# Moving the scores of one chunk between two FFN units, and spreading block loads over the first tile

## The chip, the cores and the metric

The kernel runs on one core of one Trainium2 chip. The metric is the device time of one execution in microseconds (us). Every run also has its span (first to last instruction of the core, about 1.7 us less than the time) and its mean granted TensorE clock, 1.000 being full speed. The views name the engines thus: PE is TensorE's matrix multiplication and PEld its weight load, DVE is VectorE, ACT ScalarE, POOL GpSimd, and SPq the queue of SyncE from which the transfers (DMA) are issued. PSUM is the memory in which the kernel places PE's products; a bank is here one buffer of its PSUM pools (the pool of scores and states has four).

## The reference

Retention attention over 8 batches, 8 heads, 576 positions and 64 columns, whose output becomes a 4608 x 512 matrix, followed by a maxout feed-forward network (FFN) with three weight matrices of 512 x 768 and one of 768 x 512. The FFN weights are float64.

```python
ret = scores * Dmat[None]                 # scores = q k^T / 8, Dmat: gamma_h ** (i - j), causal
x = (ret @ v).transpose(0, 2, 1, 3).reshape(4608, 512)
h = np.maximum(np.maximum(x @ w1, x @ w2), x @ w3)
return (h @ w_out).astype(np.float32)
```

## The kernel before

The tokens are cut into 36 chunks of 128 positions and into tiles of four chunks. While the FFN of tile t runs, the attention of tile t+1 is woven into it, at twelve numbered places: at each place some attention steps are emitted, then one FFN unit (a third of the products for a pair of feature blocks).

Tile 0 is special. Its units use plain products ("up"), and beside them the float64 weights are turned into float32: DVE and ScalarE take the bit patterns apart, GpSimd (POOL) makes the last product. A piece is one block of 128 x 512 weights. Conversion runs about one unit ahead of PE, and weight bits are fetched six pieces ahead. Each POOL product is followed by the load of a later piece:

```python
w_sb[piece] = ...
nc.gpsimd.tensor_tensor(w, mant[:], expo[:].bitcast(FP32), op=ALU.mult)
load_weights(1)                     # into the same queue as everything else
```

From chunk 7 on, q and k come in as blocks of 32 x 32, which DVE transposes (for chunk 7 in 0.70 and 0.66 us). That takes 32 small loads of 16 KB for each chunk, all emitted in `load(g)`:

```python
for n, src in () if g < BY_PE else (("q", q), ("kx", k)):
    t = raws[n, g] = raw.tile([P, NP, C // 32, 32], FP32, ...)
    for blk in range(C // 32):
        for a in range(4):
            nc.sync.dma_start(t[32 * a:32 * a + 32, :, blk, :], src[...])
```

The places in tile 0, for chunks 4 and 5 (`a`, `b`), and the rule for 6 and 7 that follows at places 6 to 11:

```python
if a == CPT:
    at(0, (load, b))
    at(1, (load, a + 2))
    at(2, (transposes, b), (decay_values, b))
    at(3, (scores, a), (scores, b), (load, b + 2))
    at(4, (state, a))
    at(5, (state, b))
    at(6, (values, a, b))
    continue
at(m, (transposes, a), (decay_values, a), (load, a + 2))
at(m + 1, (transposes, b), (decay_values, b))
at(m + 2, (scores, a), (scores, b), (load, b + 2))
# state a, state b, values a, b at m + 3, m + 4, m + 5
```

`scores` takes two of the four PSUM banks of one pool and two mask copies on DVE; `state` takes one bank of the same pool. After the ninth unit come four "down" products of six blocks each with w_out, then tile 1, whose units use fewer products and prepared sums.

Of the kernel before, what the change touches and what calls it, by code (L numbers as in the profile page):

```python
# [34 lines left out]
FP32 = mybir.dt.float32  # L35
# [7 lines left out]
C = 128  # L43
NT = 4 * C
NH = NT // 2
BY_PE = 7
# [5 lines left out]
def kernel(  # L52
# [15 lines left out]
    P = 128  # L68
# [3 lines left out]
    NP = H // 2  # L72
    NG = B * S // C
    NDC = DM // P
    NF = DF // P
    CPT = NT // C
# [3 lines left out]
    raw = ctx.enter_context(tc.tile_pool(name="raw", bufs=AHEAD + 1))  # L80
# [46 lines left out]
    raws, vds, qks, sts, states = {}, {}, {}, {}, {}  # L127

    def spans(g):

        row = 0
        while row < C:
            b, pos = divmod(g * C + row, S)
            n = min(C - row, S - pos)
            yield row, b, pos, n
            row += n

    def load(g, *between):
        rows = (("k", k), ("q", q), ("v", v)) if g < BY_PE else (("k", k), ("v", v))
        for n, src in () if g < BY_PE else (("q", q), ("kx", k)):  # L140

            t = raws[n, g] = raw.tile([P, NP, C // 32, 32], FP32, tag=n, name=n + "raw", bufs=3 if n == "q" else 2)
            for blk in range(C // 32):
                b, pos = divmod(g * C + 32 * blk, S)
                for a in range(4):
                    nc.sync.dma_start(
                        t[32 * a:32 * a + 32, :, blk, :],
                        src[b, a // 2::2, pos:pos + 32, 32 * (a % 2):32 * (a % 2) + 32].rearrange("p j i -> j p i"))
        for n, src in rows:
            if n == "v":  # L150
                for t, what in between:
                    nc.sync.dma_start(t[:], what)
            t = raws[n, g] = raw.tile([C, H, D], FP32, tag=n, name=n + "raw", bufs=4 if n == "k" else 3)
            for row, b, pos, m in spans(g):
                nc.sync.dma_start(t[row:row + m], src[b, :, pos:pos + m, :].rearrange("h p d -> p h d"))
# [398 lines left out]

    warm(6)
    load(0)
    load(1, (gs, state_decay), (gq, out_decay))
    load(2)
    load(3)
    load_weights(2)  # L560
# [30 lines left out]
    def steps(t):  # L591


        todo = [[] for _ in range(3 * CPT)]

        def at(n, *what):
            todo[n].extend(partial(step, *chunks) for step, *chunks in what if max(chunks) < NG)

        for n in range(0, CPT, 2):
            a, b, m = CPT * t + n, CPT * t + n + 1, 6 * (n // 2)  # L600
            if a == CPT:
                at(0, (load, b))
                at(1, (load, a + 2))
                at(2, (transposes, b), (decay_values, b))
                at(3, (scores, a), (scores, b), (load, b + 2))
                at(4, (state, a))
                at(5, (state, b))
                at(6, (values, a, b))
                continue
            at(m, (transposes, a), (decay_values, a), (load, a + 2))  # L610
            at(m + 1, (transposes, b), (decay_values, b))
            at(m + 2, (scores, a), (scores, b), (load, b + 2))
            at(m + 3, (state, a))
            at(m + 4, (state, b))
            at(m + 5, (values, a, b))
        return todo

    for t in range(N // NT):
        work = ffn(t)
        for todo in steps(t + 1):  # L620
            for step in todo:
                step()
            next(work, None)
# [51 lines left out]
```

## Time and profile before

| | before |
|---|---|
| median of the first three runs | 823.48 us |
| those three runs | 821.67, 823.48, 825.85 |
| time of the profiled execution | 826.78 us |
| its span, mean clock | 825.1 us, 0.996 |
| PE busy | 816.1 us (99%) |

A busy share of 99% does not say that PE runs at its pace: a matmul at half clock is also busy (from 38.25 to 41.66 us of this profile PE is busy for 3.41 of 3.41 us, at clock 0.50). What matters is where PE is idle, which clock it has afterwards, and which wait ends the idle time.

### The profile page before, as it was taken

Reading aid. Unit: us, or ns where it says so; the run is one execution under the profiler, and the core shown is the slowest. Engines: PE = TensorE matmul, PEld = TensorE weight load, DVE = VectorE, ACT = ScalarE, POOL = GpSimd, SP = SyncE. Lnnn points to the kernel's source line nnn. Section 1 sums busy time; section 2 is a strip of 40 time slices with the busy share of each in tenths; the row PEclk is TensorE's granted clock in tenths of the full one; section 3 lists DMA queues with packets and bytes.
Section 4 is the critical chain, followed back from the end, with each engine's and each line's share of the span. In section 5 each row is a group of like instructions: output and inputs, shape, how many; then the busy total and the mean of one; then the engine's idle time right before and its main releaser. Section 6 shows DMA issues by size and latency. Waiting matters only on the chain.

```text
span 825.1 us, 12666 instructions
## 1 busy us (share of the span) xinstructions
PE 816.1 (99%) x4616; PEld 672.7 (82%) x4616; DVE 433.2 (52%) x805; ACT 173.7 (21%) x401; POOL 191.3 (23%) x182
## 2 busy tenths in 40 slices
PE   9899999999999999999999999999999999999998
PEld 8455546888888888888888888888888888888887
DVE  4999977555353544453544445453545344533342
ACT  2766521111111102111111111111111021111211
POOL 3645468211310130111221121202111302111000
PEclk9999999999999999999999999999999999999999
DMA  9965441333233222432233413333323223001001
GB/s 244 289 176 166 101 98 48 57 56 57 83 57 56 54 63 52 80 55 59 58 55 55 86 52 57 55 56 85 58 54 56 63 52 77 1 14 39 1 1 51
DMA packets 236094, 59.33 MB, mean 72 GB/s; under 512 B 217088, under 2 KB 234496, under 8 KB 236032
## 3 DMA queue, kind: packets, MB, share of 16 engines
q1 hardware_dynamic: 235888, 58.53, 31.4%
q8 instruction: 36, 0.59, 0.3%
q14 instruction: 26, 0.21, 0.1%
q10 hardware_dynamic: 144, 0.00, 0.0%
HBM read 49.03 MB, written 9.44 MB: 71 GB/s over the span
## 4 chain that ended last, share of the span: by engine, by line
PE 88%; DVE 6%; DMA 2%; issue 2%; ACT 1%; SPq 0%; POOL 0%; DVEq 0%; POOLq 0%; ACTq 0%
PE x L456 31%; PE z L456 15%; PE dx L329 10%; PE y L456 8%; PE dz L329 5%; PE s L186 4%; PE o L221 4%; PE o L229 3%; PE kv L200 3%; PE dy L329 3%; PE down L505 2%; DVE expo L408 2%; DMA bits<-in_moe_w_out_dram 2%; DVE frac L397 1%; DVE mant L403 1%
## 5 line engine op out<-in xcount | busy, mean ns | idle before, releaser
L456 PE MATMUL x<-S,T 128*128 128x256 f32 x576 | 147.9, 379 | 0.0
L456 PEld LDWEIGHTS x<-S,T 128*128 128x128 f32 x576 | 109.1, 190 | 15.4 <-ACT u L461 0.3
L206 POOL TENSOR_TENSOR state<-state,gs 128x512 f32<-128x512 f32 x24 | 32.3, 1345 | 242.9 <-DVE state L205 239.0
L456 PE MATMUL x<-xT,w 128*128 128x256 f32 x288 | 75.6, 385 | 0.0
L486 DVE TENSOR_TENSOR tmp<-x,p 128x256 f32<-128x256 f32 x48 | 20.4, 424 | 103.5 <-PE x L456 103.5
L456 PE MATMUL x<-S,w 128*128 128x256 f32 x288 | 74.3, 380 | 0.0
L456 PE MATMUL z<-S,w 128*128 128x256 f32 x288 | 73.9, 379 | 0.0
L456 PE MATMUL z<-xT,T 128*128 128x256 f32 x288 | 73.9, 379 | 0.0
L456 PE MATMUL y<-xT,w 128*128 128x256 f32 x288 | 73.9, 379 | 0.0
L307 POOL TENSOR_TENSOR H<-h 128x256 f32<-128x256 f32 x24 | 20.6, 858 | 226.5 <-DVE h L499 226.5
L461 ACT COPY p<-x 128x256 f32<-128x256 f32 x72 | 26.8, 373 | 202.3 <-PE x L456 202.3
L514 PE MATMUL up<-xT,w 128*128 128x512 f32 x144 | 65.3, 609 | 2.2 <-POOL w L414 2.2
L233 DVE TENSOR_TENSOR xT<-o,gq 128x512 f32<-128x512 f32 x36 | 24.7, 691 | 71.8 <-PE o L229 64.9
L456 PEld LDWEIGHTS z<-S,w 128*128 128x128 f32 x288 | 54.7, 190 | 7.4
L456 PEld LDWEIGHTS y<-xT,w 128*128 128x128 f32 x288 | 54.7, 190 | 7.4
L456 PEld LDWEIGHTS z<-xT,T 128*128 128x128 f32 x288 | 54.5, 189 | 7.7
L456 PEld LDWEIGHTS x<-S,w 128*128 128x128 f32 x288 | 49.4, 189 | 13.2 <-issue 1.5
L456 PEld LDWEIGHTS x<-xT,w 128*128 128x128 f32 x288 | 52.1, 190 | 8.0 <-issue 0.5
L514 PEld LDWEIGHTS up<-xT,w 128*128 128x128 f32 x144 | 27.3, 194 | 35.3 <-issue 31.7
L189 DVE TENSOR_TENSOR st<-s,causal 128x512 f32<-128x512 f32 x72 | 44.8, 682 | 9.1 <-PE s L186 8.2
L461 ACT COPY u<-x 128x256 f32<-128x256 f32 x72 | 26.8, 372 | 100.2 <-PE x L456 95.7
L329 PE MATMUL dx<-To,H 128*128 128x256 f32 x192 | 44.2, 380 | 0.0
(92 smaller groups left out, 1200.6 us busy)
## 6 DMA issues: line engine op xcount, KB each, us to landing
bits<-in_moe_w_dram SPq DMA_DIRECT2D x18, 512.0 KB, 5.2
out_dram<-osb SPq DMA_DIRECT2D x35, 256.0 KB, 2.1
kraw<-in_k_dram SPq DMA_DIRECT2D x32, 256.0 KB, 3.0
vraw<-in_v_dram SPq DMA_DIRECT2D x32, 256.0 KB, 3.5
qraw<-in_q_dram SPq DMA_DIRECT2D x464, 16.0 KB, 1.8
kxraw<-in_k_dram SPq DMA_DIRECT2D x464, 16.0 KB, 1.8
bits<-in_moe_w_out_dram SPq DMA_DIRECT2D x6, 512.0 KB, 6.9
qraw<-in_q_dram SPq DMA_DIRECT2D x6, 256.0 KB, 4.9
```

The costliest lines, as they stand in the source:

```text
L186: nc.tensor.matmul(s[j][:, p, :], lhsT=kT[r, p, :], rhs=qT[r, p, :], start=True, stop=True)
L189: nc.vector.tensor_tensor(st[:, j], s[j][:], masks[start_of(g)][:].unsqueeze(1).to_broadcast([C, NP, C]), op=ALU.mult)
L200: nc.tensor.matmul(kv[:, p, :], lhsT=pair(kr, p)[r:], rhs=pair(vds[g], p)[r:], start=True, stop=True)
L206: nc.gpsimd.tensor_tensor(t[:], t[:], gs[:], op=ALU.mult)
L221: nc.tensor.matmul(o[g][D * j:D * (j + 1), p, :], lhsT=vr[:, 2 * p + j, :], rhs=st[:, j, p, :], start=(p == 0), stop=(before(g) == 0 and p ...
L229: nc.tensor.matmul(o[g][:, p, :old], lhsT=sd[:, p, :], rhs=qT[:, p, :old], start=False, stop=(p == NP - 1), skip_group_check=True)
L233: nc.vector.tensor_tensor(xT[t][:, :, i * C:(i + 1) * C], o[g][:], gq[:], op=ALU.mult)
L307: chores.append(lambda: (pool(s3, a11, a21, op=ALU.subtract), pool(s4, a12, s2, op=ALU.subtract)))
L329: nc.tensor.matmul(out[m], lhsT=hS[n](fp)[:, m * P:(m + 1) * P], rhs=late["T"][n][:, fp, :], start=first and fp == 0 and (m == 0 or last a ...
L456: nc.tensor.matmul(out[:], lhsT=w[:, d * P:(d + 1) * P], rhs=xS[t][n][:, d, :], start=first and d == 0, stop=d == 1, skip_group_check=True)
L461: nc.scalar.copy(c[:], src[:])
L514: nc.tensor.matmul(ps[:], lhsT=w_sb[i, fb][:, dc * P:(dc + 1) * P], rhs=xT[t][:, dc, :], start=(dc == 0), stop=(dc == NDC - 1))
```

## The change

Its intent: put PE work into the hole between the first two FFN units, and keep the block loads of chunks 7 to 9 from standing as one long piece ahead of weight loads in the queue. The helper `load_blocks(g, *blocks)` emits the loads of some blocks only; `load(g)` emits what is left.

```diff
+        if t == 1:
+            a, b, c, d = range(CPT, 2 * CPT)
+            at(0, (load, b))
+            at(1, (scores, a), (state, a))
+            at(2, (transposes, b), (decay_values, b), (load, c))
+            at(3, (scores, b), (load_blocks, d, 0))
+            at(4, (state, b), (load_blocks, d, 1, 2))
+            at(5, (values, a, b), (load_blocks, d, 3), (load, d))
+            at(6, (transposes, c), (decay_values, c), (load_blocks, d + 1, 0))
+            at(7, (transposes, d), (decay_values, d), (load_blocks, d + 1, 1, 2))
+            at(8, (scores, c), (scores, d), (load_blocks, d + 1, 3), (load, d + 1))
+            at(9, (state, c), (load_blocks, d + 2, 0, 1))
+            at(10, (state, d), (load_blocks, d + 2, 2))
+            at(11, (values, c, d), (load_blocks, d + 2, 3), (load, d + 2))
+            return todo
-            if a == CPT:
-                ... (the places shown above)
```

More of the change, by code (lines that the diff above doesn't have):

```diff
@@ L136, in spans, with load_blocks @@
             row += n
-    def load(g, *between):
-        rows = (("k", k), ("q", q), ("v", v)) if g < BY_PE else (("k", k), ("v", v))
-        for n, src in () if g < BY_PE else (("q", q), ("kx", k)):
-            t = raws[n, g] = raw.tile([P, NP, C // 32, 32], FP32, tag=n, name=n + "raw", bufs=3 if n == "q" else 2)
-            for blk in range(C // 32):
+    def load_blocks(g, *blocks):
+        for n, src in (("q", q), ("kx", k)):
+            if 0 in blocks:
+                raws[n, g] = raw.tile([P, NP, C // 32, 32], FP32, tag=n, name=n + "raw", bufs=3 if n == "q" else 2)
+            t = raws[n, g]
+            for blk in blocks:
                 b, pos = divmod(g * C + 32 * blk, S)
@@ L148, in load @@
                         src[b, a // 2::2, pos:pos + 32, 32 * (a % 2):32 * (a % 2) + 32].rearrange("p j i -> j p i"))
-        for n, src in rows:
+    def load(g, *between):
+        if g >= BY_PE and ("q", g) not in raws:
+            load_blocks(g, *range(C // 32))
+        for n, src in (("k", k), ("q", q), ("v", v)) if g < BY_PE else (("k", k), ("v", v)):
             if n == "v":
@@ L596, in at @@
         def at(n, *what):
-            todo[n].extend(partial(step, *chunks) for step, *chunks in what if max(chunks) < NG)
+            todo[n].extend(partial(step, *args) for step, *args in what if args[0] < NG)
+        if t == 1:
[13 more added lines that the diff above has]
+            return todo
         for n in range(0, CPT, 2):
             a, b, m = CPT * t + n, CPT * t + n + 1, 6 * (n // 2)
-            if a == CPT:
-                at(0, (load, b))
-                at(1, (load, a + 2))
-                at(2, (transposes, b), (decay_values, b))
-                at(3, (scores, a), (scores, b), (load, b + 2))
-                at(4, (state, a))
-                at(5, (state, b))
-                at(6, (values, a, b))
-                continue
             at(m, (transposes, a), (decay_values, a), (load, a + 2))
```

## The prediction

> **What bounds the kernel now.** I read the page first for its two busiest rows and its strips of 40 slices.
>
> ```profile
> PE 816.1 (99%) x4616; PEld 672.7 (82%) x4616; DVE 433.2 (52%) x805; ACT 173.7 (21%) x401; POOL 191.3 (23%) x182
> ...
> PE   9899999999999999999999999999999999999998
> ...
> DVE  4999977555353544453544445453545344533342
> ...
> PEclk9999999999999999999999999999999999999999
> ```
>
> PE is the bound over the whole span. DVE is full only in slices 2 to 5 (20 to 103 us), where the first tile's weights are converted. From 117 us on the timeline of PE shows matmuls back to back at a constant pace (0.43 us per 512 columns), so nothing after that can be won by moving loads. Hence I cut the first 140 us at the places where PE's timeline shows idle time, and asked for busy time and granted clock in each stretch (columns: stretch, length, busy us of PE, PEld, DVE, ACT, POOL with counts, clock, DMA share, GB/s):
>
> ```profile
> 35.00:37.15 2.15, 0.00 (x0) 0.00 (x0) 2.15 (x4) 2.12 (x5) 2.15 (x2) 1.00 0.82 172
> 37.15:45.80 8.65, 8.65 (x16) 3.69 (x17) 8.65 (x12) 5.77 (x9) 5.19 (x4) 0.80 0.95 293
> ...
> 110.55:112.44 1.89, 0.00 (x0) 0.00 (x1) 1.89 (x4) 0.00 (x0) 1.89 (x2) 1.00 0.23 35
> 112.44:117.01 4.57, 4.57 (x13) 2.61 (x13) 3.32 (x5) 0.59 (x1) 4.21 (x5) 0.63 0.23 35
> ```
>
> There are two holes, each followed by a stretch at a lower clock that a busy PE row hides. Hole 1: 2.15 us idle, then the second FFN unit's 16 matmuls take 8.67 us, where a later unit's take 6.96 (46.70 to 53.66): 1.71 lost. Hole 2: 1.89 us idle, then four down matmuls (1.73 us at full pace) and eight of the state product (0.89) take 4.57: 1.95 lost, of which about 0.36 is a second wait (the fifth block's matmuls end near 113.30, the sixth's begin at 113.66). Together 7.7 us: the ceiling of any change here, 0.9% of the time.
>
> Who ends the holes? The timelines of POOL, PE, DVE and the issuing queue say it:
>
> ```profile
> 32.90 4.20 POOL L414 TENSOR_TENSOR w<-mant,expo 128x512 f32<-128x512 f32 x1 [2.25 <-DVE expo L408]
> ```
> ```profile
> 112.44 3.29 PE L505 MATMUL down<-w_out,h 128*128 128x512 f32 x4 [1.89 <-POOL w_out L414]
> ```
> ```profile
> 79.11 0.43 DVE L392 TENSOR_SCALAR expo<-bits 128x512 int32<-128x512 int32 x1 [0.64 <-DMA bits<-in_moe_w_dram]
> ...
> 106.20 0.43 DVE L392 TENSOR_SCALAR expo<-bits 128x512 int32<-128x512 int32 x1 [2.97 <-DMA bits<-in_moe_w_out_dram]
> ...
> 107.48 0.43 DVE L392 TENSOR_SCALAR expo<-bits 128x512 int32<-128x512 int32 x1 [0.51 <-DMA bits<-in_moe_w_out_dram]
> ```
> ```profile
> 78.32 11.49 SPq L146 DMA_DIRECT2D qraw<-in_q_dram  x16
> 89.85 8.64 SPq L146 DMA_DIRECT2D kxraw<-in_k_dram  x16
> ...
> 99.70 1.39 SPq L270 DMA_DIRECT2D bits<-in_moe_w_out_dram  x2
> ```
>
> Hole 1 ends with POOL's product for the second unit's weights. Hole 2 ends with POOL's product for the fifth block of w_out, which DVE fed late because it stood for 2.97 and 0.51 us (and 0.64 us earlier) for weight bits. Those bits came late because the queue issued the 32 small block loads of chunk 8 first: the buffers of the last two w_out loads were free when DVE had done pieces 16 and 17 (84.5 and 86.8 us), but they were issued at 99.7. The chain of waits also lists 7.78 us of an earlier w_out load and 3.17 us of a block load; I discard both, since DVE's timeline has no idle time there.
>
> [...]short windows around both holes give a mean clock of 0.51 in 38.2 to 41.6 us and 0.52 in 113.5 to 116.9, about 3.4 us each; half of that is 1.7 us, the loss seen. [...]Here 16 KB block loads take 0.43 to 0.72 us of queue each while moving little: 46 GB/s in 86 to 101 us.
>
> **The change part by part.** *Scores and state of chunk 4* go between units 0 and 1, into hole 1. No instruction is added. Their cost on PE is 0.99 us (half of the 1.98 from 53.66 to 55.64) plus 1.08 (62.71 to 63.79) = 2.07 us. The inputs are ready: the transposed q and k are copied by 28.6 us, the decayed v by 28.1. They fill 2.07 of 2.15 us. The unit still starts at 37.15, but no longer at half clock: 1.71 us saved there, and 2.07 at the old places. PE leads by 3.78 us afterwards. On DVE two masked copies (0.62 each) and a state multiply (0.60) move to 41 us, before pieces 6 and 7: those come 1.9 us later, on POOL at about 48.9 and 50.7 us, while PE wants them at 53.1; pieces 8 and 9 at about 58.3, wanted at 61.0. So this delay is hidden; from the third unit on, the DVE order evens out (two mask copies fewer there), and moving the values of chunks 4 and 5 up by one unit costs 1.4 us of delay for pieces 14 and 15, which have 6 us of slack.
>
> *The block loads* of chunk 7 are spread over three places, so pieces 16 and 17 are issued near 62 us instead of 73.6: the 0.64 us stall goes. Of chunk 8 only 8 of the 32 loads stand before the last two w_out loads, which go out when their buffers are free, about 84 to 87 us, and with a landing of 6.5 us are there by 93, wanted by DVE at about 102.6. The 2.97 and 0.51 go too. Sum on DVE: 4.12 us. The fifth w_out block is then ready at 112.44 - 4.12 = 108.32, and PE, leading by 3.78, asks at 106.77: it still waits 1.55 us, and 0.36 for the sixth block, 1.9 in all against 2.25 before. Neither half is worth its own size: PE's lead alone would only make hole 2 longer. The sixth block's matmuls start at 113.66 - 4.12 = 109.54; if the clock now holds, another 1.7 us is saved by the end of the slow stretch: 5.8 us. If it drops again, the saving is 4.1. [...]I give the drop 40%. Expected saving: 0.6 x 5.8 + 0.4 x 4.1 = 5.1 us.
>
> *Chunk 9's loads* are now mixed with the output stores. A store waits in the same queue for its down matmuls, so the last blocks are issued near 117 to 122 us; they are transposed near 136 or later. That is hidden. Weight sums and x sums on DVE and POOL after hole 2 start when POOL's last w_out product ends, also about 4.1 us earlier; the last x sum is then near 126.4 us, wanted near 132. So the lead is kept into tile 1, where PE alone sets the pace to the end.
>
> **Rivals.** (1) *Everything was hidden:* the w_out bits come early [...]so hole 2 moves less than 4.1. For it: the 4.20 us case. Against: most products take 1.3 to 1.7 there. The time would be 820 to 822. (2) *DVE or POOL becomes the bound between 45 and 100 us:* PE leads by 3.8 us and conversion is 1.9 late, so some unit waits for weights. The tightest margin I find is 2.1 us (pieces 6 and 7 at 53.1), the next 1.6 (DVE waiting for the values of chunks 4 and 5 at 73.3); if one breaks, up to 2 us of the lead is lost early, but hole 2 absorbs 1.55 of that: 818 to 820. (3) *Hole 2 vanishes completely* because DVE also runs freer than I count: the ceiling, 7.7 us, 815.8. (4) *Spreading delays weights:* a weight load now stands behind block loads more often; each group costs 4 to 8 us of queue, and weights are fetched six pieces ahead, over 20 us. Small; 823 to 825.
>
> **Range and chances.** 823.48 - 5.1 = 818.4, rounded to 818.3. The three runs of before spread over 4.2 us, so I take 815.5 to 821.3: from just past the ceiling to a gain of 2.2 us. A 2% gain would need 16.5 us, twice all that the holes hold; a 2% loss would need a stall ten times the largest margin I found broken. Faster 0.01, within 2% 0.98, slower 0.01.
>
> **What would show it.** Right: PE has no hole over 0.3 us near 35 us and the clock is 1.00 in 37 to 46; the first unit after hole 1 takes 7.0 us; DVE shows no wait for bits at 78 or 103; the last two w_out loads are issued before 90 us; the wait for the fifth block begins near 107 and lasts 1 to 2 us; tile 1's first matmul starts near 130.5 to 132.3 instead of 136.34. Wrong: a new wait of PE for weights between 45 and 100 us, the state product of chunk 4 waiting so that hole 1 stays, or the lead shrinking again between 117 and 160 us.

4.12 us of waits on DVE, and 1.7 for the slow stretch if the clock holds, give 0.6 x 5.8 + 0.4 x 4.1 = 5.1 us, and 823.48 - 5.1 = 818.4. What the trace of the kernel before shows is that 2.15 and 1.89 us of idle time were each followed, 1.10 and 0.90 us after PE's restart, by 3.41 us at clock 0.50.

## The result, and the profile after

The changed kernel took 820.37 us (median of six runs, 820.01 to 821.09), the kernel before 823.80 (six runs, 821.67 to 825.85). The ratio is 0.9958, with a 95% interval of 0.9941 to 0.9975: within 2%, and clear of 1. A ratio is the mean time of one kernel's fast runs over that of the other's fast runs of the same rounds, so it is not quite the ratio of the medians. Executions over 1.5% slower than the fastest of the same kernel are left out of the means. All outputs are right.

The span of the profile fell from 825.1 to 818.6 us, by 6.5 us, nearly twice what the medians fell. That gap is the main question.

The page of the changed kernel, the same rows:

```profile
PE 811.4 (99%) x4616; PEld 670.1 (82%) x4616; DVE 432.6 (53%) x805; ACT 173.7 (21%) x401; POOL 190.9 (23%) x182
...
PE   8999999999999999999999999999999999999998
...
DVE  3999997454454535354445345553545344533341
```

The same number of matmuls has lost 4.7 us of "busy" time, and the number of instructions of no engine in this row changed: it is mostly the slow clock that has gone from PE's row (an estimate: 1.7 us for each of two drops, half of the 3.41 us at clock 0.50). The stretches of the first tile, with the columns as in the prediction:

```profile
34.91:37.15 2.24, 2.06 (x26) 1.87 (x25) 2.24 (x4) 2.21 (x5) 2.24 (x2) 1.00 0.88 190
37.15:44.12 6.97, 6.97 (x17) 3.09 (x17) 6.97 (x11) 3.26 (x6) 4.57 (x3) 1.00 0.93 291
...
106.53:108.67 2.14, 1.27 (x3) 0.30 (x2) 1.96 (x4) 0.00 (x0) 1.51 (x3) 1.00 0.24 36
108.67:110.53 1.86, 1.86 (x11) 1.38 (x11) 1.83 (x3) 0.59 (x1) 1.50 (x2) 1.00 0.01 1
```

Hole 1 is filled (PE works 2.06 of 2.24 us) and the unit after it takes 6.97 us, at clock 1.00. In hole 2 PE idles 0.87 us of 2.14, and the clock stays at 1.00. The timelines of PE, POOL and the queue:

```profile
34.91 1.16 PE L191 MATMUL s<-qT,kT 64*128 64x128 f32 x16
35.91 1.05 PE L205 MATMUL kv<-vd,kraw 64*128 64x128 f32 x8
37.15 7.13 PE L519 MATMUL up<-xT,w 128*128 128x512 f32 x16 [0.18 <-POOL w L419]
...
108.67 1.13 PE L510 MATMUL down<-w_out,h 128*128 128x512 f32 x2 [0.77 <-POOL w_out L419]
...
129.86 1.03 PE L461 MATMUL x<-xT,w 128*128 128x256 f32 x4
```
```profile
105.07 1.65 POOL L419 TENSOR_TENSOR w_out<-mant,expo 128x512 f32<-128x512 f32 x1 [4.87 <-DVE expo L413]
107.35 1.27 POOL L419 TENSOR_TENSOR w_out<-mant,expo 128x512 f32<-128x512 f32 x1 [0.63 <-DVE expo L413]
```
```profile
84.80 1.19 SPq L275 DMA_DIRECT2D bits<-in_moe_w_out_dram  x2
```

The scores and the state product of chunk 4 now stand in the hole. The last two w_out loads are issued at 84.80 us instead of 99.70, DVE shows no wait for a load between 60 and 112 us, and the last two w_out blocks are ready near 106.7 and 108.6 us. Tile 1 begins at 129.86; before, its first product stood here:

```profile
136.34 1.03 PE L456 MATMUL x<-xT,w 128*128 128x256 f32 x4
```

From there to the end of the span it is 688.76 us before and 688.74 after. All that the change does is done before tile 1, 6.48 us of it in this pair of profiles. I use the start of tile 1 as the measure of a profile from here on.

### The profile page after: what moved, and what is told of

Its sections match the earlier page's. It is cut to its first block, busy times and chain, and to the rows that moved or that the text cites. A ratio compares the mean times of both kernels' runs of the same rounds, so it can differ in the third digit from the quotient of the medians.

```text
span 818.6 us, 12678 instructions
## 1 busy us (share of the span) xinstructions
PE 811.4 (99%) x4616; PEld 670.1 (82%) x4616; DVE 432.6 (53%) x805; ACT 173.7 (21%) x401; POOL 190.9 (23%) x182
## 4 chain that ended last, share of the span: by engine, by line
PE 86%; DVE 6%; issue 2%; SPq 2%; DMA 2%; ACT 1%; POOL 0%; DVEq 0%; ACTq 0%
PE x L461 31%; PE z L461 15%; PE dx L334 10%; PE y L461 8%; PE dz L334 5%; PE o L226 3%; PE s L191 3%; PE o L234 3%; PE kv L205 3%; PE dy L334 3%; PE down L510 2%; DVE expo L413 2%; DVE frac L402 1%; SPq L160 1%; DVE mant L408 1%
## 5 line engine op out<-in xcount | busy, mean ns | idle before, releaser
L519 PE MATMUL up<-xT,w 128*128 128x512 f32 x144 | 63.5, 595 | 0.2 <-POOL w L419 0.2
L480 DVE TENSOR_TENSOR tmp<-y,p 128x256 f32<-128x256 f32 x48 | 20.4, 424 | 45.3 <-PE y L461 39.3
```

What stands on the lines that cost most here:

```text
L519: nc.tensor.matmul(ps[:], lhsT=w_sb[i, fb][:, dc * P:(dc + 1) * P], rhs=xT[t][:, dc, :], start=(dc == 0), stop=(dc == NDC - 1))
```

## The experiments

Twelve runs were made, each timed in five rounds beside the kernel before: the first four (the kernel before again, and the next three below) on one chip, the other eight on another. Theory: PE's lead and the readiness of the last w_out blocks form a minimum, each half of the change being worth little alone, and the difference between 6.5 and 3.4 us is the clock, which drops in some executions of the kernel before and not in others. Rivals are stated with each run.

### The kernel before, again

No edit.

> The kernel before, unchanged, to see each run's granted clock. The gain between the two profiles is 6.5 us (825.1 to 818.6), between the medians only 3.4. Theory A: the profile of before caught both clock drops (mean clock 0.996), and most runs have fewer[...]; then the runs spread over about 4 us, those with a clock near 1.000 are the fast ones (about 821.5 to 822.5), those at 0.996 the slow ones (825 to 827), and the clock explains the order. Theory B: the clock is 0.996 in nearly every run, and the spread comes from when the late w_out loads land; then time and clock do not go together.

It took 824.81 us (822.37 to 826.84). With the eleven runs of before made beside it on that chip, and the twelve on the other, there are 29 runs whose clock is known:

| mean clock | runs | mean us | range |
|---|---|---|---|
| 1.000 | 8 | 822.93 | 821.73 to 823.96 |
| 0.998 | 17 | 824.08 | 822.76 to 825.49 |
| 0.995, 0.996 | 4 | 827.05 | 826.74 to 827.41 |

The order is that of the clock, as theory A has it, and the first profile (826.78 us, 0.996) belongs with the slowest 4 of 29. Its new profile has clock 0.998. PE's timeline in it:

```profile
37.15 8.83 PE L514 MATMUL up<-xT,w 128*128 128x512 f32 x16 [2.16 <-POOL w L414]
...
111.45 1.12 PE L505 MATMUL down<-w_out,h 128*128 128x512 f32 x2 [0.91 <-POOL w_out L414]
113.35 1.12 PE L505 MATMUL down<-w_out,h 128*128 128x512 f32 x2 [0.77 <-POOL w_out L414]
...
134.54 1.03 PE L456 MATMUL x<-xT,w 128*128 128x256 f32 x4
```

Hole 1 and its slow unit (8.83 us) are as before. Hole 2 idles 1.68 us, and its products run at full pace (1.12 us for two; the clock is 1.00 in 105 to 118 us). Tile 1 starts at 134.54, 1.80 us sooner than in the first profile. There, the products of the sixth w_out block were these:

```profile
113.66 2.07 PE L505 MATMUL down<-w_out,h 128*128 128x512 f32 x2
```

From the start of the sixth block's products to tile 1 it is 21.19 us here (113.35 to 134.54), as in the changed kernel (108.67 to 129.86), and 22.68 in the first profile. So 1.49 of the 1.80 us is the clock drop after hole 2, and 0.31 is the block itself.

Theory B holds in part as well. The last two w_out loads were issued 1.20 us later than in the first profile, but DVE's wait for the first of them ended 0.51 us sooner:

```profile
100.90 1.40 SPq L270 DMA_DIRECT2D bits<-in_moe_w_out_dram  x2
```
```profile
105.69 0.43 DVE L392 TENSOR_SCALAR expo<-bits 128x512 int32<-128x512 int32 x1 [1.12 <-DMA bits<-in_moe_w_out_dram]
```

From the issue of the two loads to the end of that wait it is 4.79 us, against 6.50 in the first profile (99.70 to 106.20). And the lost clock alone does not give the eight runs at clock 1.000: without any drop, a run of 822.93 us began the sixth block's products near 111.3 us (an estimate: 822.93 less 1.71 outside the span, 688.76 and 21.19), 2.1 us before this profile did, where PE stood idle for that block. In those runs the block itself must have been ready sooner. No execution of before with clock 1.000 was profiled, so what made it ready sooner stays open.

### The scores alone

```diff
-at(1, (scores, a), (state, a))        # as in the changed kernel
+at(1, (scores, a), (state, a), (load, c))
 ... block loads, state of chunk 5 and values of 4 and 5 as in the kernel before
```

> Scores and state product of chunk 4 moved between the first two units; all block loads as before. My theory: hole 1 is filled and the lead of PE is 2 to 3.8 us before the down matmuls, but the fifth w_out block is ready no earlier (about 112.4 us), so hole 2 grows to 4 to 6 us, and the end moves by 0 to 0.5 us: ratio 0.9995 to 1.0005 against the kernel before, at most 0.999. Rival (the halves add up): the lead stays, 2 to 3.8 us faster, ratio 0.9955 to 0.9975.

825.12 us (821.48 to 826.10), ratio 1.000 (0.9974 to 1.0025). The lead is there and worth nothing:

```profile
110.61 3.97 PE L510 MATMUL down<-w_out,h 128*128 128x512 f32 x4 [4.89 <-POOL w_out L419]
...
134.71 1.03 PE L461 MATMUL x<-xT,w 128*128 128x256 f32 x4
```

PE waits 4.89 us for the fifth w_out block in one piece, four products then take 3.97 us (two take 1.12 at full pace), and tile 1 starts at 134.71, 0.17 us later than in the second profile of before. The mean clock is 0.71 in 105.72 to 110.61 us and 0.58 in 110.61 to 115.38, which makes half clock from about 107.8 to 114.6 us (an estimate from these means), in one stretch that begins within the wait. This one stretch makes the mean clock 0.996, so 0.996 alone does not show two separate drops. The rival, that the halves add up, falls.

### The loads alone

```diff
-at(1, (scores, a), (state, a))
-at(3, (scores, b), (load_blocks, d, 0))
+at(3, (scores, a), (scores, b), (load_blocks, d, 0))
 ... states and values at the places of the kernel before, all block loads as in the change
```

> Block loads spread as in the change; scores and state product of chunk 4 at their old places. My theory: DVE never waits for w_out bits, the fifth block is ready near 107 us, PE asks for it near 110.5 (hole 1 with its clock drop is still there) and does not wait: hole 2 is gone, the end moves by 2.25 us of idle time and, where the clock dropped there, 1.7 more: 2 to 4 us in the profile, ratio 0.996 to 0.998, with runs of clock 0.998 (a drop after hole 1) and 1.000. Rival (the loads do nothing alone, since DVE had slack): ratio 1.000 and hole 2 as before.

822.83 us (820.99 to 823.50), ratio 0.9975 (0.9955 to 0.9996). In its profile the first six down products run without a gap:

```profile
107.02 5.32 PE L510 MATMUL down<-w_out,h 128*128 128x512 f32 x12
...
132.39 1.03 PE L461 MATMUL x<-xT,w 128*128 128x256 f32 x4
```

Hole 2 is gone and only hole 1 is left, with a mean clock of 0.63 in 37.0 to 41.6 us, which makes 3.4 us at half clock (an estimate). This makes it the cleanest measure of one clock drop, though from few runs: the two runs at 1.000 took 820.99 and 821.38 us, the four at 0.998 took 822.72 to 823.50. The means, 821.19 and 823.11, differ by 1.9 us, where half of these 3.4 us is 1.7. The rival (the loads do nothing alone) falls.

### Chunk 8 in one piece ahead of the last two w_out loads

```diff
-at(6, ..., (load_blocks, d + 1, 0))
-at(7, ..., (load_blocks, d + 1, 1, 2))
-at(8, ..., (load_blocks, d + 1, 3), (load, d + 1))
+at(6, ..., (load, d + 1))
+at(7, ...)
+at(8, ...)
```

> The changed kernel, but all 32 block loads of chunk 8 stand in one piece before the last two w_out loads, as in the kernel before; chunks 7 and 9 spread. My theory: the place of chunk 8 against the last two w_out loads is what matters, so DVE waits again for 2.5 to 4 us near 102 us, hole 2 is 4 to 6 us long with PE's lead, and nearly all of the gain is lost: ratio to before 0.999 to 1.000, tile 1 begins 3.5 us or more later than in the changed kernel. Rival (spreading as such, or chunk 7's place, gives the gain): ratio stays near 0.996.

824.13 us (823.85 to 825.34), ratio 0.9997. DVE waits for the bits again, and so does PE for the blocks:

```profile
104.15 0.43 DVE L397 TENSOR_SCALAR expo<-bits 128x512 int32<-128x512 int32 x1 [1.15 <-DMA bits<-in_moe_w_out_dram]
```
```profile
108.49 1.13 PE L510 MATMUL down<-w_out,h 128*128 128x512 f32 x2 [1.74 <-POOL w_out L419]
110.38 2.08 PE L510 MATMUL down<-w_out,h 128*128 128x512 f32 x2 [0.77 <-POOL w_out L419]
...
133.02 1.03 PE L461 MATMUL x<-xT,w 128*128 128x256 f32 x4
```

DVE's two waits sum to 1.46 us, less than the 2.5 to 4 that I expected, since the loads went out at 96.70 us and not at 99.7. Yet hole 2 idles 2.51 us, the clock is 0.998 in all six runs, and two products take 2.08 us instead of 1.12 (clock 0.55 in 110.38 to 113.69 us). Nearly all of the gain is lost by this one edit. The rival falls.

### The changed kernel, again (two runs of the study)

No edit; each is the base for runs.

> The changed kernel, unchanged, as the base for the next runs on this chip. All runs at clock 1.000 and within about 1 us of each other (820.0 to 821.1 the first time), if its two holes are too short to drop the clock; [...]some runs show 0.998 and take up to 1.7 us more.

> The changed kernel again, as the base on this chip: 819.3 to 821.1 in single runs, clock 1.000 (once 0.999 so far).

(The last part of the first text is for the case that the holes are not too short.) 820.21 us (819.25 to 820.36) and 819.98 us (819.18 to 821.22). With the first six runs that makes 17, of mean 820.15: 16 at clock 1.000 and one at 0.999. The run at 0.999 was profiled: its clock is 1.00 in every stretch asked for from 178 to 800 us, and its products in hole 2 take 1.12 us for two; where the clock fell was not shown. The waits that are left are together 0.8 to 1.3 us near 107 us in the lists of three profiles, and the products after them run at full pace in each.

### Only the scores in hole 1, the state product later

```diff
-at(1, (scores, a), (state, a))
+at(1, (scores, a))
-at(3, (scores, b), ...)
+at(3, (scores, b), (state, a), ...)
```

> The changed kernel, with only the scores of chunk 4 in hole 1 and its state product later, before the fourth unit. Hole 1 is then about 1.26 us instead of 0.18 and PE's lead 1.08 us smaller. My theory: time is set by when the last w_out block is ready, PE arrives there with about 1 us to spare in the changed kernel, so the time stays within 0.3 us of it, provided the hole of 1.26 us drops no clock (clock 1.000 in all runs). Rivals: PE's lead counts in full, 1.1 us slower; or the clock drops after 1.26 us in some runs (0.998), these are 1 to 2 us slower.

820.07 us (819.09 to 820.82), against 820.21 for the changed kernel, all six at clock 1.000:

```profile
37.05 7.13 PE L519 MATMUL up<-xT,w 128*128 128x512 f32 x16 [1.08 <-POOL w L419]
...
108.72 1.12 PE L510 MATMUL down<-w_out,h 128*128 128x512 f32 x2 [0.39 <-POOL w_out L419]
```

Hole 1 idles 1.08 us instead of 0.18, and the wait for the sixth block shrinks from 0.77 to 0.39; its products start at 108.72, against 108.43 in the profile of the base. Tile 1 starts at 129.91 against 129.62. So the last 0.9 us of PE's lead buy at most 0.3 us in the profile and nothing in the medians; with 1.08 us of idle time in hole 1 the clock stayed at 1.000 in all six runs. The rival that the lead counts in full falls.

### Chunk 8 in one piece after the last two w_out loads

```diff
-at(6, ..., (load_blocks, d + 1, 0))
-at(7, ..., (load_blocks, d + 1, 1, 2))
-at(8, ..., (load_blocks, d + 1, 3), (load, d + 1))
+at(6, ...)
+at(7, ..., (load, d + 1))
+at(8, ...)
```

> The changed kernel, but all 32 block loads of chunk 8 in one piece one place later, after the last two w_out loads instead of around them. My theory: only the order against these two loads matters, not the parts: time within 0.3 us of the changed kernel, DVE without a wait for w_out bits. Rival (spreading in parts is what frees the queue): slower by 1 us or more.

821.08 us (820.55 to 822.23), 0.9 above the base, so my number missed. But up to tile 1 the two profiles are alike: tile 1 begins at 129.63 us here and at 129.62 in the base, and neither DVE shows a wait for bits. The 0.8 us by which the spans differ come later: twice, near 183 and 760 us, a PE weight load waits 0.5 us for a sum on DVE that began late, for no reason that the profile shows. All five runs are slower than all five of the base, so the waits are hardly chance; what makes the two late sums stays open, and the edit does not touch their instructions. So order against these two loads is enough for the gain before tile 1.

### Chunk 7 in one piece

```diff
-at(3, (scores, b), (load_blocks, d, 0))
-at(4, (state, b), (load_blocks, d, 1, 2))
-at(5, (values, a, b), (load_blocks, d, 3), (load, d))
+at(3, (scores, b), (load, d))
+at(4, (state, b))
+at(5, (values, a, b))
```

> The changed kernel, with the block loads of chunk 7 in one piece as in the kernel before; chunks 8 and 9 spread. My theory: DVE waits again for the weight bits of the ninth unit near 78 us, 0.6 to 2.9 us as in the profiles of before, the last w_out blocks come that much later, and PE's wait for them grows by as much: 0.6 to 2.9 us slower than the changed kernel, in some runs with a clock drop (0.998). Rival (only chunk 8 counts): within 0.3 us of it.

820.47 us (820.35 to 820.82), against 819.98 for the base. The wait is back:

```profile
79.55 0.54 DVE L397 TENSOR_SCALAR expo<-bits 128x512 int32<-128x512 int32 x1 [2.50 <-DMA bits<-in_moe_w_dram]
```

With a second one of 0.48 it makes 2.98 us, but tile 1 starts only 0.47 us later (130.22 against 129.75). In the first profile of the changed kernel DVE does these four mask instructions at once while POOL makes two products, and they take 0.89, 1.51, 1.27 and 0.41 us (in the base they take 1.11, 1.26, 0.41 and 0.41, and the product step before them 1.75 instead of 0.67); after the wait POOL has ended its two products, and they take 0.54, 0.41, 0.43 and 0.42. The four steps thus take 1.80 us instead of 3.19 in the base, and the product step 0.68 instead of 1.75: 2.46 of the 2.98 us of waiting come back in shorter steps. I had expected 0.6 us at least.

### Chunk 9 in one piece

```diff
-at(9, (state, c), (load_blocks, d + 2, 0, 1))
-at(10, (state, d), (load_blocks, d + 2, 2))
-at(11, (values, c, d), (load_blocks, d + 2, 3), (load, d + 2))
+at(9, (state, c), (load, d + 2))
+at(10, (state, d))
+at(11, (values, c, d))
```

> The changed kernel, with the block loads of chunk 9 in one piece ahead of the first output store. My theory: chunk 9's part plays no role, as its data are wanted by DVE only near 136 us and the first store can wait: within 0.3 us of the changed kernel, the first store issued about 4 us later. Rival (the store in the queue holds an output buffer): a wait of PE or ScalarE for a down buffer between 115 and 135 us, slower by 0.5 us or more.

820.92 us (four fast runs, 819.94 to 821.17). Tile 1 starts at 129.70 us, within 0.05 of the base, though the first store is issued at 117.29 instead of 110.34 us: spreading chunk 9 is worth nothing before tile 1. The median is 0.9 above the base, and again two waits of 0.5 us for late sums on DVE stand in its profile, at the same two places (183 and 760 us); none of the twelve profiles of the other kernels has them. So this number missed too, by the same unexplained event.

### Two tries at the waits that are left

First, the scores of chunks 6 and 7 one place later:

```diff
-at(8, (scores, c), (scores, d), ...)
+at(8, ...)
-at(9, (state, c), ...)
+at(9, (scores, c), (scores, d), (state, c), ...)
```

> The changed kernel, with the scores of chunks 6 and 7 one place later, after the ninth FFN unit instead of before it. Their four mask copies (2.4 us on DVE) then stand after the conversion of the last two w_out blocks. In the changed kernel PE waits 0.25 and 0.77 us for these blocks, as DVE's order decides when they are ready. My theory: both waits go, the end comes 0.8 to 1.1 us earlier: about 819.4, every run below the changed kernel's median. Rival: the mask copies delay the weight sums and the values of chunks 6 and 7, a new wait takes the place: 820.4 or more.

825.94 us (824.62 to 826.62), ratio 1.0024: slower than before.

```profile
106.97 2.07 PE L205 MATMUL kv<-vd,kraw 128*128 128x128 f32 x8 [5.26 <-DVE st L194]
```

The scores hold all four PSUM banks of their pool, their mask copies now come after the conversion, and the state product waits 5.26 us for a bank; the eight products then take 2.07 us, where the next eight take 1.05, and the twelve after them 6.61, where the next twelve take 5.32. The mean clock of the profiled run is 0.996. I had looked for waits on mask copies, and not for banks.

Second, only the scores of chunk 7 later:

```diff
-at(8, (scores, c), (scores, d), ...)
+at(8, (scores, c), ...)
-at(9, (state, c), ...)
+at(9, (scores, d), (state, c), ...)
```

> Second try at the last two waits of the changed kernel. The first try put the scores of both chunks late and lost 5.7 us, since all four score banks were held and the state product waited 5.26 us for a bank. Now only the scores of chunk 7 come after the ninth unit; chunk 6 stays before it and frees its banks in time. DVE then converts the last two w_out blocks 1.2 us earlier (two mask copies fewer ahead), ready near 105.5 and 107.4 instead of 106.7 and 108.6, and PE asks at 106.5 and 107.4. My theory: no wait over 0.3 us in hole 2, 0.8 to 1.0 us faster than the changed kernel: 819.2 to 819.5. Rival (a bank or the mask copies of chunk 7 make a new wait): same time or slower.

```profile
103.52 5.32 PE L510 MATMUL down<-w_out,h 128*128 128x512 f32 x12
...
128.90 1.03 PE L461 MATMUL x<-xT,w 128*128 128x256 f32 x4
```

Both waits are gone: twelve matmuls in 5.32 us, tile 1 at 128.90 against 129.75 in the base, the 0.85 us expected. The time is 819.64 us (818.56 to 821.64), against 819.98 (819.18 to 821.22): five runs at clock 1.000, and the slowest at 0.998. So its profile beats both kernels, but the timed runs do not separate it from the changed one.

## Why the prediction was right or wrong

**The bound and the two holes: right.** Hole 1, hole 2 and what ends them were as read, and nothing after them mattered: it is 688.74 us from the start of tile 1 to the end, against 688.76.

**Scores and state into hole 1: right.** 0.18 us of idle time are left (0.08 expected), the unit takes 6.97 us (7.0). No new wait came up between 45 and 100 us, so rival 2 did not happen.

**The loads: right in mechanism, the term on DVE too small.** Pieces 16 and 17 and the last two w_out loads went out when I said, and the waits went. I summed 4.12 us from the waits alone. The fifth block's last DVE step ended at 110.05 us before and at 104.99 after, 5.06 us earlier, and its POOL product took 1.65 us instead of 2.26. Most of the rest was there before hole 2: DVE's transposes of chunk 7 began at 91.21 us instead of 92.60, 1.39 us earlier, where the wait that went explains 0.64. DVE's steps beside POOL's products took other times: of the steps ahead of the transposes, two that took 1.75 us before took 0.67, and the POOL product beside the second of them took 2.26 us instead of 1.65. A single step differs between executions (the second took 1.75 in a third profile of the changed kernel), but the sum holds: these transposes began at 90.98 to 91.21 us in three profiles of the changed kernel, at 92.60 and 92.94 in two of the kernel before. Why the steps took other times was not shown; no run tests it. (Most of POOL's products take 1.3 to 1.7 us.) The delay of pieces 6 and 7 was too large as well: POOL ended them at 47.7 and 49.6 us, 0.7 later than before and not 1.9. PE therefore waited about 0.25 us for the fifth block, not 1.55, and 0.77 for the sixth, not 0.36. So two of the signs missed: the wait for the fifth block was to last 1 to 2 us, and tile 1 to start at 130.5 to 132.3 (129.86). Experiment "chunk 7 in one piece" shows the same thing from the other side.

**Neither half worth its own size: right.** The scores alone gave nothing (ratio 1.000), the loads alone about half (0.9975), both 0.9958. The change also moves the values of chunks 4 and 5 up by one unit, and both halves left them at the old place; no run tests that part by itself.

**The clock after the change: the 40% for a drop was too high.** In 17 runs no run is below 0.999. This, and DVE's shorter steps (0.67 us for 1.75, twice), make the saving in the profile 6.5 us where I expected 5.1, and 5.8 at best.

**Where it failed: the base.** The step is "823.48 - 5.1 = 818.4": I worked the savings out on one execution, and took them off the median of others. The profiled execution took 826.78 us, 3.3 us above that median, and its clock of 0.996 was a sign of it: it had both drops. I counted the loss at half clock as if every execution had it, "half of that is 1.7 us, the loss seen". Of the 29 runs of before, 4 had a mean clock this low, 17 had 0.998 and 8 had 1.000. But the clock is at most half of the 3.3 us: the drop after hole 2 was worth 1.49 us, and PE's lost time after hole 1 ended in hole 2, where PE waited for POOL anyway. The other 1.8 us (an estimate, the difference) is that the w_out blocks came later in the profiled execution than in a median one. Taken off the profile's own time, the measured 6.5 gives 820.3, which is what was measured (820.37). Taken off the median, the saving is 3.4 us. So the prediction's two errors, a saving in the profile 1.4 us too small and a base 3.3 us too fast for that saving, partly cancelled. The time fell inside the range, 2 us above its centre; that the errors have opposite signs is luck. (A slip besides: 818.4 was "rounded" to 818.3.)

**The rivals.** Rival 1 (820 to 822 us, hole 2 moves less) names the right time for a wrong reason: hole 2's blocks came more than 4.1 us earlier, not less. Rivals 3 and 4 did not happen: hole 2 was left with about 1 us, and no weight came late.

**What stays open.** Which part of the time differences of before is the drop itself and which is the earlier block in the runs without a drop; how much idle time, and when, is followed by a drop; why the bits land sooner in some executions; and the late sums on DVE of two variants.

## What to carry to other kernels

Before a saving is read from a profile, compare the profiled execution's own time and clock with the timed runs, and take the saving off the same execution; a part that depends on the clock is worth only its share of the runs. Where two engines meet at one point, an earlier arrival of one is worth no more than the other's readiness allows (here the scores alone gave a ratio of 1.000, the loads alone 0.9975, both 0.9958): change both, and test each half alone. When a queue carries bulk loads and urgent ones, look first at which urgent load stands behind the bulk: here the order counted before tile 1, and the cutting into parts of chunk 8 did not.

## What was measured of the clock and of DVE, and was not explained

- In the first profile the two slow stretches are 3.41 us long each, at clock 0.50, from about 38.25 and 113.34 us, and the 3.41 us just ahead of each hold 2.15 and 1.89 us of idle time. The cases show no rule for what idle time is followed by a drop. With the holes as in the profile of each variant and the mean clock of each run, one hole of 2.16 us went with a drop in four of six runs (the loads alone), holes of 1.74 and 0.77 us within 3.6 us in six of six (chunk 8 in one piece ahead), while with 1.08 us in hole 1 no run of six had one (the state product later), with 0.64 and 0.77 us within 2.5 us none of five (chunk 7 in one piece), and with 0.8 to 1.3 us none of 17 runs was below 0.999. A drop costs 1.9 us of 821, measured between two runs without it and four with it, of one kernel.
- In the first profile of the changed kernel a mask step on DVE took 1.51 us beside POOL's product, and in the run with chunk 7 in one piece 0.41 after it. There a wait of 2.98 us for data cost 0.47, as DVE's steps then ran after POOL's products and were shorter.
- The late sums of 0.5 us on DVE, in a steady stretch of the kernel, have no explanation here.
